# Keeping four engines of a DeltaNet and FFN kernel in program order, with the first stages regrouped

## The chip, the cores and the metric

One core of a Trainium2 chip runs the whole kernel. Time is device microseconds (us) of that core. Runs of one kernel agree within about one per cent. Kernels are compared only within the same rounds. The kernel before took 722.61 us (median of three runs, 721.08 to 725.26).

In the profile PE is TensorE (matmuls), PEld its weight loads, DVE is VectorE, ACT is ScalarE, POOL is GpSimd, SP is SyncE, whose queue here issues most DMAs. A line of an order of time reads: start in us, duration in us, engine, source line, operation, out<-in, shape, count, and in brackets the idle time just before it with what ended that.

## The reference

Two stages on 4 batches, 8 heads, 768 tokens, head size 48 (model width 384):

```python
k_n = k / (np.linalg.norm(k, axis=-1, keepdims=True) + 1e-06)
for t in range(S):                       # attention: a delta rule, token by token
    y[:, :, t] = einsum('bhd,bhde->bhe', q[:, :, t], state)
    v_old = einsum('bhde,bhd->bhe', state, kt)
    state = state + bt * einsum('bhd,bhe->bhde', kt, vt - v_old)
# x = y with the heads side by side, [4, 768, 384]
xn = (x - mean) / sqrt(var + 1e-06) * g_ln
out = x + maximum(xn @ w_ch1, 0.0) @ w_ch2      # 384 -> 1536 -> 384
```

The weights come as float64.

## The kernel before

The sequence is cut into 12 chunks of 64 tokens; two chunks make a slab. The program is written as Python generators, and a `Plan` decides in which order their steps are put out: `spread(gen, count, t0, t1)` puts the steps of a generator evenly between two points of a made-up time axis ("steps of the plan", meant to be about a microsecond). After that a scheduler is still free to reorder the instructions of each engine.

The parts that matter:

```python
def to_fp32(i):            # one "weight piece", 128x384 doubles: 6 VectorE instructions
    part  = (hi >> 13) & 0x3FF80
    power = max(part, ..) - ..
    man   = hi & 0xFFFFF | 0x100000
    full  = lo * 2**-32 + man
    full  = hi & 0x80000000 | full
    w_sb  = full * scale_w * power
# 24 pieces: 12 of w1, then 12 of w2

def prep(c):               # k, q transposed (p_t), gram matrices (p_g -> gsb, pt), gsb to DRAM (gd)
def blocks(m, engs):       # inverse of the diagonal blocks of a slab
    for ...: dma(gb, gd)                    # 8 small transfers back from DRAM
    yield
    nrm = sqrt(diagonal of gb)              # ScalarE: the "norms"
    nrm = 1/(nrm + 1e-6); db = nrm*nrm*beta; gb = gb*db; ...   # VectorE
    yield
    for j in range(31):                     # 31 pairs, each needs the one before
        tmp = xb[column j] * gb[row j]
        xb  = xb - tmp
        if j % 2: yield
    dma(xd, xb); for ...: dma(xt, xd)
    yield
def join(chunks):          # xn = transpose(xt) on VectorE; p_e, p_z on TensorE, ScalarE between
def recur(c, g):           # p_by, rhs, p_u, u, p_s, s, p_by, x_ln, LayerNorm (xn_ln), p_n
def ffn(c):                # 12 x (3 p_h, h_f); then, for each token group, 12 p_o

# ... the first stages (see the diff), then:
T = 45
starts = [0, 16, 84] + [114 + T * i for i in range(NCH - 2)]
plan.spread(join(range(2)), 5, -1, 0)
plan.spread(weights(6, NW // 2), NW // 2 - 6, 0, 20)
plan.spread(weights(NW // 2, NW), NW - NW // 2, 20, 52)
for c in range(NCH):
    plan.spread(in_turn(recur(c, 0), recur(c, 1)), 2 * N_RECUR, starts[c], ends[c])
...                                          # ffn(0): 12 to 32 and 48 to 64; ffn(1): 64 to 114
for c in range(2, NCH):
    plan.spread(ffn(c), N_FFN, starts[c + 1], starts[c + 1] + T)
for m in range(1, NSL):                      # slabs 1 to 5
    times = (t - 88, t - 62, t - 26, t - 8) if m > 1 else (4, 22, 62, 76)
    plan.spread(in_turn(*(prep(c) for c in chunks)), SLAB * N_PREP, times[0], times[1])
    plan.spread(blocks(m, (nc.sync,)), N_BLOCKS + 1, times[1], times[2])
    plan.spread(join(chunks), 5, times[3], t)
plan.run()
```

## Time and profile before

| what | us |
|---|---|
| first join (first xn on VectorE) | 107.2 |
| FFN of chunk 0 starts | 133.8 |
| second join (first p_e) | 201.9 |
| end of the trace | 719.1 |
| TensorE idle from 201.9 to the end | 37.9 |

This is the list of TensorE's waits of the kernel before from 201.9 to the end; the columns are us in total, times, and the longest.

```profile
PE p_e L392 <- DVE xn L384: 16.8, 4, 11.9
PE p_s L475 <- ACT u L432: 3.5, 5, 0.9
PE p_n L513 <- DVE xn_ln L506: 3.0, 4, 1.1
```

The one large wait is for the transposed inverse at the joins. The other waits of the list last at most 1.5 us each; they come to 16.9 us in sum, and the last matmul ends at 714.5, 4.6 us before the end.

### The profile page before, as it was taken

To read this page: it belongs to the slowest core of one execution; us is meant where nothing else is said; L and a number is where in the kernel's file an instruction comes from. 1 tells how busy PE (TensorE), PEld (TensorE's weight loads), DVE (VectorE), ACT (ScalarE), POOL (GpSimd) and SP (SyncE) were. 2 spreads that over 40 slices of the span, in tenths; PEclk is the share of its full clock that TensorE was granted. 3 is DMA by queue.
4 is the path that set the end of the run, shared out by engine and by line. 5 is a ranking of instruction groups with operands and counts; after the bars stand their busy time and mean duration, and the time that the engine had idled before them with its cause. 6 is when DMAs were issued, how large, how long until landed. Compare 5 with 4: busy or idle time off the path is not lost.

```text
span 719.1 us, 17676 instructions
## 1 busy us (share of the span) xinstructions
PE 586.0 (81%) x7784; PEld 433.2 (60%) x7784; DVE 355.7 (49%) x894; ACT 179.4 (25%) x452; POOL 59.9 (8%) x80
## 2 busy tenths in 40 slices
PE   1610008999998994799998899997999999999997
PEld 1410007776865762686765786765876757858684
DVE  4788997337735297311497313595212874021100
ACT  3200003531233221233221352222341312213120
POOL 5222440001000011000011000011000000000000
PEclk9999999999999898599999699998799997999999
DMA  8998261433034412113505023414012012000000
GB/s 148 199 192 143 71 168 47 90 75 60 30 64 101 68 34 68 28 30 91 79 3 122 7 64 70 67 25 103 2 46 56 14 45 39 1 12 13 12 12 22
DMA packets 135292, 45.28 MB, mean 63 GB/s; under 512 B 128304, under 2 KB 131376, under 8 KB 135216
## 3 DMA queue, kind: packets, MB, share of 16 engines
q1 hardware_dynamic: 126992, 33.80, 24.4%
q0 software_dynamic: 1920, 9.44, 4.7%
q10 hardware_dynamic: 6304, 0.92, 1.0%
q8 instruction: 61, 1.00, 0.6%
q14 instruction: 15, 0.12, 0.1%
HBM read 29.98 MB, written 14.16 MB: 61 GB/s over the span
## 4 chain that ended last, share of the span: by engine, by line
PE 54%; DVE 30%; DMA 7%; issue 3%; ACT 3%; SPq 2%; POOL 0%; DVEq 0%; ACTq 0%; POOLq 0%
PE p_h L526 19%; PE p_o L537 17%; DVE tmp L357 9%; DVE xb L362 8%; PE p_t L249 3%; PE p_g L260 3%; PE p_by L448 2%; DMA words<-in_moe_w_ch_dram 2%; PE p_z L412 2%; PE p_u L464 2%; PE p_e L392 2%; PE p_by L490 2%; SPq L116 1%; PE p_n L513 1%; PE p_s L475 1%
## 5 line engine op out<-in xcount | busy, mean ns | idle before, releaser
L526 PE MATMUL p_h<-xnt,w_sb 128*128 128x256 f32 x864 | 213.3, 397 | 1.3 <-ACT h_f L531 1.1
L537 PE MATMUL p_o<-w_sb,h_f 128*128 128x384 f32 x576 | 200.9, 494 | 0.0
L526 PEld LDWEIGHTS p_h<-xnt,w_sb 128*128 128x128 f32 x864 | 164.6, 198 | 28.7 <-ACT h_f L531 2.5
L537 PEld LDWEIGHTS p_o<-w_sb,h_f 128*128 128x128 f32 x576 | 104.9, 190 | 62.1 <-issue 0.5
L531 ACT ACTIVATE h_f<-p_h 128x256 f32<-128x256 f32 x144 | 55.0, 383 | 148.6 <-PE p_h L526 148.3
L392 PE MATMUL p_e<-xn,gsb 32*32 32x32 f32 x768 | 20.7, 218 | 73.3 <-DVE xn L384 73.3
L357 DVE TENSOR_TENSOR tmp<-xb,gb 128x31 f32<-128x31 f32 (+15 forms) x186 | 67.0, 360 | 4.3
L362 DVE TENSOR_TENSOR xb<-xb,tmp 128x31 f32<-128x31 f32 (+15 forms) x186 | 64.2, 345 | 4.5
L392 PEld LDWEIGHTS p_e<-xn,gsb 32*32 32x32 f32 x768 | 18.5, 132 | 76.6 <-DVE xn L384 73.0
L268 DVE TENSOR_TENSOR pt<-p_g,pmask 128x512 f32<-128x512 f32 x24 | 16.6, 690 | 79.7 <-ACT gsb L265 78.0
L260 PE MATMUL p_g<-kqt 48*64 48x128 f32 (+1 forms) x896 | 31.2, 287 | 26.6 <-DVE nrm L342 15.3
L260 PEld LDWEIGHTS p_g<-kqt 48*64 48x64 f32 x896 | 25.0, 157 | 34.2 <-ACT ksq L280 15.4
L544 DVE TENSOR_TENSOR o<-p_o,x_ln 128x384 f32<-128x384 f32 x24 | 13.4, 557 | 61.4 <-PE p_o L537 61.1
L481 DVE TENSOR_TENSOR s<-s,p_s 48x384 f32<-48x384 f32 x44 | 24.3, 552 | 23.7 <-PE p_s L475 23.0
L448 PEld LDWEIGHTS p_by<-s,kqt 48*64 48x64 f32 x1408 | 26.7, 143 | 13.1 <-issue 9.8
L453 DVE TENSOR_TENSOR rhs<-v_raw,p_by 128x384 f32<-128x384 f32 x22 | 12.1, 552 | 43.7 <-PE p_by L448 40.8
L400 ACT ACTIVATE es<-p_e 32x256 f32<-32x256 f32 x48 | 18.0, 375 | 61.4 <-PE p_e L392 55.7
L448 PE MATMUL p_by<-s,kqt 48*64 48x48 f32 x1408 | 31.5, 231 | 2.0 <-ACT x_ln L432 2.0
L250 ACT COPY kqt<-p_t 128x512 f32<-128x512 f32 x48 | 27.9, 585 | 19.2 <-PE p_t L249 12.6
L417 DVE COPY xt<-p_z 32x256 f32<-32x256 f32 x48 | 20.0, 417 | 25.3 <-PE p_z L412 24.8
L280 ACT ACTIVATE ksq<-kpad 128x384 f32<-128x384 f32 x24 | 12.5, 521 | 67.9 <-DVE ksum L281 51.1
L351 POOL COPY xb<-db 128x32 f32<-128x32 f32 x6 | 3.5, 584 | 273.9 <-DVE db L346 273.9
(68 smaller groups left out, 516.1 us busy)
## 6 DMA issues: line engine op xcount, KB each, us to landing
words<-in_moe_w_ch_dram POOLq DMA_DIRECT2D x24, 384.0 KB, 3.9
gd<-gsb SPq DMA_DIRECT2D x12, 512.0 KB, 3.2
qpad<-in_q_dram SPq DMA_DIRECT2D x24, 192.0 KB, 4.8
v_raw<-in_v_dram SPq DMA_DIRECT2D x24, 192.0 KB, 5.2
out_dram<-o SPq DMA_DIRECT2D x48, 96.0 KB, 2.2
kpad<-in_k_dram SPq DMA_DIRECT2D x22, 192.0 KB, 3.9
xd<-xb SPq DMA_DIRECT2D x6, 512.0 KB, 2.9
gb<-gd SPq DMA_DIRECT2D x44, 64.0 KB, 3.3
```

Source lines behind the costliest of these rows:

```text
L249: nc.tensor.transpose(p_t[:, j], src[:, h : h + 2], ident)
L250: nc.scalar.copy(made[c][0][g][:, :, n], p_t)
L260: nc.tensor.matmul(p_g[toks, hp, j, n0:n1], kqt[rows, j, 0, toks], kqt[rows, j, n0:n1, toks])
L357: nc.vector.tensor_tensor(out=t, in0=xb[:, 0:n, j : j + 1].to_broadcast([128, n, w]), in1=gb[:, j : j + 1, j + 1 : BK].to_broadcast([128, ...
L362: nc.vector.tensor_tensor(out=rest, in0=rest, in1=t, op=ALU.subtract)
L392: nc.tensor.matmul(p_e[r1, h % H], gsb[r0, h, BK:C], xn[r0, h])
L417: nc.vector.tensor_copy(out=xt[r0, g * H : (g + 1) * H, BK:C], in_=p_z[r0])
L448: nc.tensor.matmul(p_by[half(e ^ (hp & n)), hp, n, j], kqt[rows, j, n, half(e)], s[rows, e, j], start=(n == 0 and j == 0), stop=(n == 0), ...
L481: nc.vector.tensor_tensor(out=new, in0=new, in1=p_s[DP * hp : DP * hp + D, :, 0 : NP * D].rearrange("p e (j d) -> p e j d", d=D), op=ALU.add,)
L526: nc.tensor.matmul(p_h, w1_sb[:, t, f * 128 : (f + 1) * 128], xnt[:, t], start=(t == 0), stop=(t == KC - 1),)
L531: nc.scalar.activation(h_f, p_h, ACTF.Relu)
L537: nc.tensor.matmul(p_o, hs[f][:, g * 128 : (g + 1) * 128], w2_sb[:, f], start=(f == 0), stop=(f == FT - 1),)
```

## The change

The intent: the plan is made with care, so let the engines keep it. A context manager chains every instruction of VectorE, ScalarE, TensorE and the SyncE queue to the one before it on the same engine, with a dependency that the scheduler has to respect (GpSimd stays free). The first stages are regrouped to be good in just that order: the squares of k after the grams, only three weight pieces before the first inverse and none inside it, then values, products and the first join at once.

```diff
+@contextmanager
+def in_this_order(tc):
+    traced = tc.nc.cur_bb.bb.instructions
+    first = len(traced)
+    yield
+    last = {}
+    for ins in tc.nc.cur_bb.bb.instructions[first:]:
+        if ins.engine not in ORDERED:            # DVE, Activation, PE, SP
+            continue
+        if ins.engine in last:
+            tc.add_manual_dep(ins, last[ins.engine],
+                mybir.DependencyInfo(NoSync, DATA), reason="in_this_order")
+        last[ins.engine] = ins.name
...
-    first.spread(weights(0, 5), 5, 0, 8)
-    first.run()
-    inverse = blocks(0, (nc.sync, nc.scalar))
-    next(inverse)
-    ...                                   # loads of q and v of chunks 0, 1
-    for _ in inverse:
-        pass
-    ...                                   # prep_p of chunks 0, 1 (scale_v on GpSimd, q transposed, products)
-    first.spread(weights(5, 6), 1, 3, 4)
+    order.enter_context(in_this_order(tc))
+    first.spread(weights(0, 3), 3, 0, 8)
+    first.run()
+    knrms = [norms(c) for c in two]
+    inverse = blocks(0, (nc.sync, nc.scalar))
+    next(inverse)
+    ...                                   # loads of q and v of chunks 0, 1
+    next(inverse)
+    ...                                   # q transposed; loads of chunks 2, 3
+    for _ in inverse:
+        pass
+    for c in two:
+        scale_v(c, knrms[c], nc.vector)
+        for g in two:
+            products(c, g, 1, 2)
+    for _ in weights(3, 5):
+        pass
+    for _ in join(two):
+        pass
...
-    plan.spread(join(range(2)), 5, -1, 0)
-    plan.spread(weights(6, NW // 2), NW // 2 - 6, 0, 20)
+    plan.spread(weights(5, NW // 2), NW // 2 - 5, 0, 20)
...
     plan.run()
+    order.close()
```

## The prediction

> **What bounds the kernel now.** I read the page first (busy shares, the 40 slices), then the six stretches below, then the order of time within them.
>
> ```profile
> PE 586.0 (81%) x7784; PEld 433.2 (60%) x7784; DVE 355.7 (49%) x894; ACT 179.4 (25%) x452; POOL 59.9 (8%) x80
> ...
> PE   1610008999998994799998899997999999999997
> ...
> DVE  4788997337735297311497313595212874021100
> ...
> PEclk9999999999999898599999699998799997999999
> ```
>
> TensorE (PE) is nearly idle for the first 108 us and nearly full later; VectorE (DVE) is the reverse. The share of 81% hides two programs with two limits. The stretches, columns PE, weight load, DVE, ACT, POOL busy, granted clock, DMA share, GB/s:
>
> ```profile
> 0.00:36.10 36.10, 14.75 (x224) 11.78 (x224) 21.63 (x47) 11.61 (x21) 13.07 (x31) 1.00 0.89 173
> 36.10:50.30 14.20, 1.13 (x32) 0.97 (x32) 10.81 (x27) 0.77 (x2) 2.29 (x6) 1.00 1.24 193
> 50.30:96.90 46.60, 1.13 (x32) 0.97 (x32) 44.79 (x127) 1.90 (x5) 19.46 (x15) 1.00 0.55 114
> 96.90:133.80 36.90, 22.53 (x550) 19.07 (x550) 26.01 (x58) 9.78 (x25) 3.10 (x5) 1.00 0.43 100
> 133.80:201.90 68.10, 67.08 (x710) 50.38 (x708) 38.10 (x96) 20.65 (x52) 4.73 (x6) 1.00 0.30 64
> 201.90:719.10 517.20, 479.33 (x6242) 350.06 (x6242) 214.33 (x542) 134.72 (x348) 17.21 (x19) 0.93 0.21 44
> ```
>
> At 36.1 the norms of the first blocks exist (ACT nrm); DVE takes them up at 48.0 because weight pieces stand ahead of them. From 50.3 to 96.9 DVE runs the first inverse (31 pairs tmp, xb) interleaved one for one with ten weight pieces. The first join starts at 107.2, the FFN of chunk 0 at 133.8, with all weights converted. From there PE is full but for some waits: in the last stretch it is idle 517.2-479.3 = 37.9 us and then cold (clock 0.50 for some 10 us after each of four joins).
>
> Costs of single things are read from the order of time:
>
> ```profile
> 97.21 0.42 DVE L206 TENSOR_SCALAR part<-words 128x384 uint32<-128x384 uint32 x1
> 97.67 0.38 DVE L211 TENSOR_SCALAR power<-part 128x384 uint16<-128x384 uint32 x1
> ...
> 101.14 0.50 DVE L206 TENSOR_SCALAR part<-words 128x384 uint32<-128x384 uint32 x1 [0.85 <-DMA words<-in_moe_w_ch_dram]
> ...
> 371.13 0.42 DVE L357 TENSOR_TENSOR tmp<-xb,gb 128x255 f32<-128x255 f32 x1
> 371.58 0.42 DVE L362 TENSOR_TENSOR xb<-xb,tmp 128x255 f32<-128x255 f32 x1
> ...
> 352.68 2.86 PE L526 MATMUL p_h<-xnt,w_sb 128*128 128x256 f32 x12
> 355.46 0.68 PE L464 MATMUL p_u<-rhs,xt 64*64 64x48 f32 x32
> 356.08 2.86 PE L526 MATMUL p_h<-xnt,w_sb 128*128 128x256 f32 x12
> ...
> 335.31 0.34 SPq L305 DMA_DIRECT2D gd<-gsb  x1
> ...
> 338.32 2.29 SPq L335 DMA_DIRECT2D gb<-gd  x4
> ```
>
> A weight piece alone costs 101.14-97.21-0.85 = 3.07 us. A dependent inverse instruction costs its duration plus 0.036; the whole inverse alone is (67.0+64.2)/6 + 62*0.036 = 24.1 us. Interleaved, ten pieces and the inverse (30.7+24.1+4 ksum) took 46.6: neighbours that don't depend on each other overlap by nearly 0.1 us. A p_h record costs 1.30/6 = 0.2155 us in a run, a p_o record 0.3225, so one FFN is 72*0.2155+48*0.3225 = 31 us, and each return to the FFN from small matmuls about 0.2 more (2.78 against 2.59).
>
> **What the Trainium skill says.** "TensorE: Matmul & The Clock Gate", the table at its head: TensorE's queue is 64 deep and can only pull weight loads ahead; VectorE, ScalarE and GpSimd are strict FIFO. The trace agrees: the norms of 36.1 waited until 48.0 behind pieces that needed their own words. So the order of issue decides, and that is what changes. "VectorE: DVE Perf Modes", section "The DRAIN you can't avoid": the next op starts only when the pipe is empty, but one that isn't held starts earlier. The trace shows the difference as 3.07 us against about 2.3 us a piece. "TensorE: Matmul & The Clock Gate", Part 1: an idle window of about 3.4 us halves the clock; the trace agrees (0.50 and 0.56 at 280 to 300, after 10 us idle). "DMA: Bandwidth & Descriptors", anatomy section: about 2 us fixed per transfer; here gb took 2.7 to 5.6 us, so gd and then gb cost 8 to 9 us from the copy to use.
>
> **The change part by part.** The edges forbid the scheduler to reorder PE, DVE, ACT and the SP queue; POOL stays free. No arithmetic is removed. Two scale_v move from POOL to DVE.
>
> First stages. ACT no longer puts the squares first, so the grams go out near 18 instead of 24.9, but the gb transfers of ACT's queue stand behind the norms of k, which wait for three pieces and four ksum on DVE (about 27). Norms at about 35, hardly better than 36.1. Then DVE goes on at once: 2.4 + 24.1 = 61.5 for the inverse, against 96.9. Next, on DVE's own order, scale_v 2*0.95, four pt with a gram each between (p_g is single-buffered), two pieces 6.1: 13.8, so xn at 75.3 (before: 107.2). Here 32 us are won. The join in strict order alternates PE, ACT, DVE four times with a cold PE: about 13.5, against 10.7. The recurrence starts at about 88.8.
>
> The bill. Nineteen pieces (5 to 23) remain and now stand between the recurrences of chunks 0 and 1 and the second inverse. Piece 23 comes after pair 24 of that inverse. DVE from 88.8: 19*3.07 = 58.3; 24 pairs 19.9; norms and gb 2.3; four recurrence halves 14.0; rhs, ksum, pt 6.4; sum 100.9, less 3 for overlap, plus about 9 for waits on PE and ACT (u, s, rstd): 107. Last weight at 196. PE reaches p_o of chunk 0 at about 160, and each of its twelve steps needs one w2 piece, so it trickles to 196; the second token group takes 24*0.3225 = 7.7: 204. The second join starts at about 212 behind 18 p_h; before it started at 201.9, with nearly all of chunk 1's FFN already done.
>
> The rest. From 204 PE has 11*31 = 341 FFN, 10 chunks of recurrence at 6.26 = 62.6, prep of 8 chunks 30, joins 22, and 159 returns to the FFN at 0.2 = 32: 487.6. The same count for before from 201.9 gives 9+310+62.6+28+22+124*0.2 = 456; measured were 517.2, less 37.9 idle, less about 24 for cold stretches = 455. The count holds to a per cent. So 204+490 = 694 plus waits.
>
> Waits. In the new order norms follow the last p_g of a slab by a few positions, while the data need gsb 0.8, gd 3, gb issue 2.3, gb 3: 9.3 us. On chunk 2, rhs stands behind norms on DVE: PE has 7.2 us of work and p_u comes at 12.7. For later slabs p_n follows a LayerNorm that stands behind norms, gb, s and ten pairs; DVE gets there at 20, PE at 14. With DVE's backlog (34 us of work for 30 to 37 of PE) I get 14 us for the second slab and 13 for each of three more, cold clock included, and 1.5 elsewhere: 54. The joins themselves become nearly free, since p_o is kept back between their steps. I take three quarters, 41, as such walks count each wait in full. 694+41 = 735.
>
> **Rivals.** (a) The gain carries through: join 23 us or more earlier, the rest as before: 696. For it: chunk 0 does start earlier, and before's four cold joins go. Against: the 19 pieces; DVE was the full engine of 50 to 107 and its work isn't less. (b) Strict order smooths PE so well that waits fall to 20: 714. For: between joins before ran 10.00 of 10 us busy in much this order. Against: the 9.3 us to norms, which the scheduler had hidden by placing them 20 us after gsb (334.7 to 354.6). (c) Waits in full and a slower weight phase: 755 to 760. For: DVE and PE now wait on each other with nothing to slip in.
>
> **Range and chances.** Last weight 196 +-7, waits 41 +-15: 708 to 760 for 8 in 10, middle 735. Over 2% faster means below 708.2: needs both at their best, 0.12. Slower by over 2% means above 737.1: 0.46. Within: 0.42.
>
> **What would show it.** Right: first xn near 75; inverse without weight instructions between, some 24 us; last w_sb write near 196; PE busy under half from 90 to 195; second join after 205; idle PE before p_u or p_n just after each norms; no cold joins. Wrong: last w_sb well before 180; p_o of chunk 0 not trickling; norms without idle PE, which would give (b); or PE full from 130 on, which would give (a).

## The result, and the profile after

The changed kernel took 761.31 us (757.49 to 763.1, four runs) beside 723.79 us of the kernel before on the same chip (721.08 to 725.26). The ratio is 1.0516, 95% interval 1.0461 to 1.0571: slower. Ratios here and below are the mean time of one kernel's fast runs over that of the other's fast runs of the same rounds, so they are not quite the ratio of the medians quoted.

First the busy shares and slices of the page after:

```profile
span 760.3 us, 17663 instructions
...
PE   4102358462689769989969999599999599999997
...
DVE  3496667789613278333395423692331963221100
...
PEclk9965559876599989999989999899999899999999
```

TensorE starts earlier than before and is then half busy until slice 11 (209 us; slices count from 0), where before it was full from slice 6 (108 us). Later on there are four slices marked 5 or 6 (from 266, 380, 475 and 589 us), where the kernel before had one, marked 4, from 270 us.

The same cuts as in the prediction, placed at the events of the changed kernel (columns: stretch and its length, then busy time and count of PE, weight load, DVE, ACT, POOL, then granted clock, DMA share, GB/s):

```profile
0.00:33.90 33.90, 8.27 (x144) 6.92 (x144) 13.10 (x29) 9.83 (x17) 11.66 (x28) 1.00 0.75 145
33.90:73.20 39.30, 7.83 (x144) 6.58 (x144) 33.20 (x86) 2.34 (x4) 1.31 (x3) 0.60 0.97 125
73.20:85.00 11.80, 6.76 (x288) 5.98 (x288) 4.83 (x12) 3.01 (x8) 1.17 (x2) 0.50 0.13 36
85.00:199.80 114.80, 57.42 (x747) 41.23 (x747) 91.58 (x210) 21.06 (x55) 13.34 (x22) 0.69 0.29 73
199.80:211.50 11.70, 11.70 (x27) 6.71 (x28) 4.03 (x16) 0.00 (x0) 0.95 (x1) 0.74 0.42 98
211.50:760.30 548.80, 489.57 (x6436) 347.96 (x6434) 218.97 (x549) 139.47 (x368) 17.66 (x23) 0.96 0.26 46
```

The granted clock of the first stretches should not be compared with the 1.00 that the prediction shows for the kernel before: there p_s on 32 matmuls took 0.89 us at 118.65, against 0.57 at full clock (in the changed kernel at 370.06), so TensorE ran at half speed where the view says 1.00.

Up to 85 us the change does what it was made for: the norms are there at 33.9, the inverse runs alone, the first join starts at 73.2 instead of 107.2. Then the bill: for 115 us TensorE is half idle, while VectorE has 92 us of work. In the last stretch, TensorE is idle 548.80-489.57 = 59.2 us; before, 37.9 after 201.9.

The order of time on TensorE at the end of the fourth stretch shows why it stands:

```profile
179.74 1.65 PE L551 MATMUL p_o<-w_sb,h_f 128*128 128x384 f32 x2 [5.45 <-DVE w_sb L249]
184.38 1.65 PE L551 MATMUL p_o<-w_sb,h_f 128*128 128x384 f32 x2 [2.99 <-DVE w_sb L249]
...
199.78 11.69 PE L551 MATMUL p_o<-w_sb,h_f 128*128 128x384 f32 x26 [4.55 <-DVE w_sb L249]
...
222.38 0.69 PE L406 MATMUL p_e<-xn,gsb 32*32 32x32 f32 x32 [0.27 <-ACT kqt L271]
```

Each pair of p_o waits for one w2 piece. The last group is 26 matmuls (2 of the first token group, 24 of the second). It lasts 11.69 us, where 26 at the 0.3225 us of the prediction would last 8.4: the granted clock in it is 0.74 on average, 0.50 up to 206.0 and 1.00 after that. The second join starts at 222.4, before at 201.9.

TensorE's waits from 222 to the end, the same columns as before:

```profile
PE p_n L527 <- DVE xn_ln L520: 27.3, 7, 8.2
PE p_u L478 <- DVE rhs L467: 6.6, 2, 6.3
PE p_s L489 <- DVE pt L289: 4.3, 3, 1.4
PE p_h L540 <- ACT h_f L545: 3.9, 4, 1.0
PE p_n L527 <- ACT es L414: 3.6, 4, 0.9
PE p_t L270 <- ACT es L414: 2.6, 2, 1.7
PE p_g L281 <- DVE s L495: 1.3, 1, 1.3
PE p_e L406 <- DVE xn L398: 1.3, 4, 0.3
```

The wait for xn at the joins is gone from the top of the list (it is 1.3 us, before 16.8). In its place stands p_n, which waits for the LayerNorm. Five long waits, all soon after the norms of a slab, come to 32.5 us: two at the second slab, shown next, and one at each of the three later ones (7.29 us at 386.67, 7.85 at 491.83, 8.22 at 599.05).

```profile
269.53 1.10 PE L478 MATMUL p_u<-rhs,xt 64*64 64x48 f32 x32 [6.29 <-DVE rhs L467]
...
282.00 0.55 PE L527 MATMUL p_n<-ident,xn_ln 128*128 128x128 f32 x3 [2.80 <-DVE xn_ln L520]
```

The first of the later ones, in the order of time of all engines from 365 to 388:

```profile
365.92 0.34 SPq L329 DMA_DIRECT2D gd<-gsb  x1
...
366.36 5.75 SPq L349 DMA_DIRECT2D gb<-gd  x8
...
375.21 0.26 ACT L355 ACTIVATE nrm<-gb 128x32 f32<-128x32 f32 x1 [6.74 <-DMA gb<-gd]
...
375.51 0.18 DVE L356 TENSOR_SCALAR nrm<-nrm 128x32 f32<-128x32 f32 x1 [7.38 <-ACT nrm L355]
...
386.14 0.48 DVE L520 TENSOR_SCALAR xn_ln<-x_ln,mv,rstd 128x384 f32<-128x384 f32 x1
...
386.67 0.90 PE L527 MATMUL p_n<-ident,xn_ln 128*128 128x128 f32 x3 [7.29 <-DVE xn_ln L520]
```

Read it from the top. The grams go to DRAM and come back; that takes 375.2-365.9 = 9.3 us. VectorE stands for 7.4 us, because the norms are next in its order. The LayerNorm stands behind them and behind the first pairs of the inverse, and TensorE, with the p_n of that LayerNorm next in *its* order, stands for 7.3 us in turn. The label of a wait names only the last link (xn_ln); the first cause is the transfer three links back. The second is the work that VectorE, once it goes on at 375.5, still does ahead of the LayerNorm: the rest of the norms, the product of gb, s, o and eight pairs.

### The profile page after: what moved, and what is told of

Read it like the earlier page. It is cut to its first block, busy times and chain, and to the rows that moved or that the text cites. A ratio compares the mean times of both kernels' runs of the same rounds, so it can differ in the third digit from the quotient of the medians.

```text
span 760.3 us, 17663 instructions
## 1 busy us (share of the span) xinstructions
PE 581.5 (76%) x7784; PEld 415.4 (55%) x7784; DVE 365.7 (48%) x896; ACT 175.7 (23%) x452; POOL 46.1 (6%) x78
## 3 DMA queue, kind: packets, MB, share of 16 engines
q1 hardware_dynamic: 126992, 33.80, 26.7%
## 4 chain that ended last, share of the span: by engine, by line
PE 50%; DVE 32%; DMA 7%; ACT 4%; issue 3%; SPq 2%; ACTq 0%; DVEq 0%
PE p_o L551 19%; PE p_h L540 16%; DVE xb L376 7%; DVE tmp L371 7%; PE p_g L281 3%; DMA gb<-gd 3%; PE p_by L462 2%; DVE full L242 2%; DMA gd<-gsb 2%; DVE w_sb L249 2%; DMA kpad<-in_k_dram 2%; DVE full L245 2%; DVE s L495 2%; PE p_t L270 2%; SPq L349 2%
## 5 line engine op out<-in xcount | busy, mean ns | idle before, releaser
L551 PE MATMUL p_o<-w_sb,h_f 128*128 128x384 f32 x576 | 218.4, 521 | 21.4 <-DVE w_sb L249 21.4
L540 PEld LDWEIGHTS p_h<-xnt,w_sb 128*128 128x128 f32 x864 | 162.0, 195 | 32.0 <-ACT h_f L545 6.1
L551 PEld LDWEIGHTS p_o<-w_sb,h_f 128*128 128x128 f32 x576 | 108.4, 200 | 88.4 <-DVE w_sb L249 21.5
L371 DVE TENSOR_TENSOR tmp<-xb,gb 128x31 f32<-128x31 f32 (+15 forms) x186 | 63.2, 340 | 5.0
L281 PE MATMUL p_g<-kqt 48*64 48x128 f32 (+1 forms) x896 | 32.5, 295 | 30.2 <-DVE pt L289 23.7
L527 PE MATMUL p_n<-ident,xn_ln 128*128 128x128 f32 x72 | 14.6, 320 | 49.1 <-DVE xn_ln L520 45.6
L558 DVE TENSOR_TENSOR o<-p_o,x_ln 128x384 f32<-128x384 f32 x24 | 13.4, 557 | 59.9 <-PE p_o L551 59.7
L527 PEld LDWEIGHTS p_n<-ident,xn_ln 128*128 128x128 f32 x72 | 9.3, 159 | 55.7 <-DVE xn_ln L520 43.8
L270 PE MATMUL p_t<-ident,qpad 128*128 128x128 f32 x96 | 17.0, 313 | 21.7 <-DMA qpad<-in_q_dram 20.3
L271 ACT COPY kqt<-p_t 128x512 f32<-128x512 f32 x48 | 28.0, 584 | 20.6 <-PE p_t L270 20.0
L431 DVE COPY xt<-p_z 32x256 f32<-32x256 f32 x48 | 20.0, 417 | 22.1 <-PE p_z L426 21.4
L406 PEld LDWEIGHTS p_e<-xn,gsb 32*32 32x32 f32 x768 | 16.1, 114 | 22.0 <-DVE xn L398 9.8
L406 PE MATMUL p_e<-xn,gsb 32*32 32x32 f32 x768 | 19.0, 201 | 11.5 <-DVE xn L398 10.3
L478 PE MATMUL p_u<-rhs,xt 64*64 64x48 f32 x704 | 15.8, 230 | 15.3 <-DVE rhs L467 14.6
```

What stands on the lines that cost most here:

```text
L270: nc.tensor.transpose(p_t[:, j], src[:, h : h + 2], ident)
L271: nc.scalar.copy(made[c][0][g][:, :, n], p_t)
L281: nc.tensor.matmul(p_g[toks, hp, j, n0:n1], kqt[rows, j, 0, toks], kqt[rows, j, n0:n1, toks])
L371: nc.vector.tensor_tensor(out=t, in0=xb[:, 0:n, j : j + 1].to_broadcast([128, n, w]), in1=gb[:, j : j + 1, j + 1 : BK].to_broadcast([128, ...
L406: nc.tensor.matmul(p_e[r1, h % H], gsb[r0, h, BK:C], xn[r0, h])
L431: nc.vector.tensor_copy(out=xt[r0, g * H : (g + 1) * H, BK:C], in_=p_z[r0])
```

## The experiments

The kernels marked as edits "of the changed kernel" differ from it only by the lines shown.

### Which half of the change costs: the regrouping or the order

Regrouping without the order, an edit of the changed kernel:

```diff
-    order.enter_context(in_this_order(tc))
```

> The regrouped first stages, but no order edges: the scheduler may reorder every engine. Theory A (the strict order costs the time): the scheduler puts weight pieces between the instructions of the first inverse again, nine or ten of them, so the time is near that of the kernel before: 710 to 732 us, first xn near 100 to 107 us. Theory B (the regrouping pushed 19 pieces behind the first join and that costs the time): 745 us or more, last weight after 180 us.

The order without the regrouping: the kernel before, with the same context manager around its own first stages and plan.

```diff
+    order = ExitStack()
+    order.enter_context(in_this_order(tc))
     first = Plan()
     ...
     plan.run()
+    order.close()
```

> The kernel before with the order edges alone, its first stages as they were. Theory A: slower much like the full change, 745 to 775 us, with PE idle before p_u or p_n after each norms of slabs 2 to 5, and no weight piece between the instructions of the first inverse. Theory B: near the kernel before, 715 to 735 us.

Measured: regrouping alone 721.75 us (ratio 0.997, interval 0.9914 to 1.0026), order alone 761.12 us (1.0503, 1.0442 to 1.0565). The weight pieces show what is behind this. These are VectorE's writes of w_sb (ns min/median/max, then the first and last start in us), first of regrouping alone, then of order alone:

```profile
L249 DVE SCALAR_TENSOR_TENSOR w_sb<-full,scale_w,power x24: 602/614/1829, 15.9 to 121.5; 128x384 f32<-128x384 f32 x24
```

```profile
L249 DVE SCALAR_TENSOR_TENSOR w_sb<-full,scale_w,power x24: 617/619/619, 14.4 to 199.6; 128x384 f32<-128x384 f32 x24
```

Without the order the scheduler puts the pieces back into the first inverse whatever the source says, and they are done at 122; the first join is then at 106.5. With the order the last one starts at 199.6, and the first join starts at 78.0 even without the regrouping. So the whole loss belongs to the order, and so does most of the early start; the regrouping on its own does nothing that the interval can tell from zero.

### Where in the program the order costs

The order is kept on one side of step 64 of the plan, the step where the FFN of chunk 1 begins. Edits of the changed kernel:

```diff
# order up to the second join
-    plan.run()
-    order.close()
+    plan.once(64, order.close)
+    plan.run()

# order after it
-    order.enter_context(in_this_order(tc))
...
+    plan.once(64, order.enter_context, in_this_order(tc))
     plan.run()
     order.close()
```

> The changed kernel with its order kept only up to the step where the FFN of chunk 1 begins (step 64 of the plan); after that the scheduler is free. Theory (about half of the 38 us is the weight phase before the second join, about half the later slabs): last w_sb near 199 as in the changed kernel, p_e of the second join near 220, total 735 to 748. Rival (the later slabs cost all of it, since work put off in the weight phase is made up for by the free joins): 720 to 730.

> The reverse: the scheduler is free up to step 64 of the plan and the order is kept from there to the end. Theory: first join late (near 107) and last w_sb near 122 as without an order, the waits at the norms of the slabs come back (p_u and p_n on VectorE, 5 to 7 us at each), but the four joins run without long waits; total 735 to 748. Rival (the weight phase costs all): 720 to 728.

Measured: up to step 64, 738.67 us (1.022, 1.0171 to 1.0269), so 14.5 us over the 724.19 of before in these rounds; after it, 745.93 us (1.0306, 1.0253 to 1.0359), so 21.7 us over. Together 36.2, against 37.5 for the whole: the cost splits into two parts that add up.

The second part has waits of both sorts, those of the norms and one at the second join, which the expectation had not (TensorE's waits from 190 on):

```profile
PE p_n L527 <- DVE xn_ln L520: 26.1, 7, 7.7
PE p_e L406 <- DVE xn L398: 18.8, 5, 17.5
PE p_u L478 <- DVE rhs L467: 6.7, 1, 6.7
```

### The two costs repaired, one by one and together

Norms later. In slabs 2 to 5 the transfers of gb stay where they were, and the norms and the inverse come six steps later. An edit of the changed kernel:

```diff
-        plan.spread(blocks(m, (nc.sync,)), N_BLOCKS + 1, times[1], times[2])
+        inverse = blocks(m, (nc.sync,))
+        plan.spread(inverse, 1, times[1], times[1] + 2, whole=False)
+        late = 6 if m > 1 else 0
+        plan.spread(inverse, N_BLOCKS, times[1] + 2 + late, times[2] + late)
```

> The changed kernel, with norms and inverse of slabs 2 to 5 put out 6 plan units later than the transfers they wait for. If ACT and DVE stand in line behind the gb transfers (my theory for the waits of the later slabs): PE's idle time before p_u and p_n after norms, some 6 to 9 us a slab, goes, with its cold clock; about 35 us in all: 720 to 735 us. If the waits come from VectorE's backlog of inverse work instead, they only move: gain under 10 us, 752 us or more.

Measured 740.75 us (1.023, 1.0179 to 1.0282): 20.6 us won, but the expected time was missed by 6 us. TensorE's waits from 221 on show about half of the time for xn_ln (27.3 us) still there:

```profile
PE p_n L527 <- DVE xn_ln L520: 14.0, 11, 2.9
PE p_h L540 <- ACT h_f L545: 8.1, 4, 2.1
```

The long waits for xn_ln (up to 8.2 us each) are gone; eleven of up to 2.9 us remain, and the wait for h_f has doubled. In one of the eleven (p_n at 397.3) VectorE had copied x_ln at 392.3 and began its LayerNorm only at 395.5, with pairs of the inverse between.

Weights early. Ten weight pieces go into the first inverse, instruction by instruction, as the scheduler had done. An edit of the changed kernel, with the generators made to yield after every instruction:

```diff
-        for _ in inverse:
-            pass
+        pieces_too = weights_fine(3, 13)
+        for _ in inverse:
+            next(pieces_too, None)
+        for _ in pieces_too:
+            pass
...
-        for _ in weights(3, 5):
-            pass
...
-    plan.spread(weights(5, NW // 2), NW // 2 - 5, 0, 20)
-    plan.spread(weights(NW // 2, NW), NW - NW // 2, 20, 52)
+    plan.spread(weights(13, NW), NW - 13, 0, 40)
```

> The changed kernel, with ten weight pieces put instruction by instruction between those of the first inverse, in strict order; eleven pieces remain after the first join. If the serial weight pieces after the join hold back the FFN (my theory for the first 210 us): first xn later, near 92 us instead of 73, but last weight near 177 instead of 199.6 and no p_o that waits for w_sb; 735 to 750 us. Rival: the late join shifts all that follows and gives the gain back: 756 to 765 us.

Measured 751.42 us (1.0387, 1.0335 to 1.044): 9.9 us won, a little less than expected. The first xn moves from 73.2 to 86.4, the last w_sb from 199.0 to 182.1, and TensorE's wait for w_sb shrinks from 21.4 us in six waits to 0.9 in one. So a first join 13 us later made the kernel faster.

Both:

> Both repairs at once: norms six steps later in the slabs from the second on, and ten weight pieces inside the first inverse. Theory (two separate costs, one in the later slabs and one in the weight phase): the gains add, 20.6 + 9.9, so 761.3 - 30.5 = 731, within 726 to 736. Rival (both are one stock of slack of TensorE, which can be won back only once): 738 to 742, no better than norms late alone.

Measured 732.62 us (1.015, 1.0099 to 1.0201): 28.7 us below the changed kernel, against 20.6+9.9 = 30.5. Two separate costs, repaired separately.

### Which engine's order costs

Edits of the one line that names the ordered engines:

```diff
-ORDERED = tuple(getattr(mybir.EngineType, n) for n in ("DVE", "Activation", "PE", "SP"))
+ORDERED = tuple(getattr(mybir.EngineType, n) for n in ("DVE",))           # or ("PE",), or ("DVE", "PE")
```

> The changed kernel with the order kept on VectorE alone; TensorE, ScalarE and the queue are left to the scheduler. Theory (VectorE's place for the norms and for the weights is the cause; TensorE's own order only decides whether it can fill the wait): last w_sb late, 185 to 200, as in the changed kernel, but TensorE slips FFN matmuls into the waits of p_n and p_u, so 730 to 748. Rival (the cost is TensorE's rigid order): within 1.5% of the kernel before, 715 to 728.

> The order kept on TensorE alone. Theory (VectorE's order is the cause): with VectorE free the scheduler puts weight pieces inside the first inverse and the norms where their data are there, so last w_sb near 122 to 130, waits at norms under 10 us in sum, 715 to 730. Rival (TensorE's rigid order is the cause): 745 or more, with p_n and p_u waits as in the changed kernel.

> The order kept on TensorE and VectorE, with ScalarE and the queue left to the scheduler. Alone the order of VectorE cost 2 us and that of TensorE 11. Theory (the cost is the product of the two: VectorE late by its own order, and TensorE unable to fill the wait by its own): nearly the whole of it, 752 to 764. Rival (the order of ScalarE or of the queue, which neither of those runs had, makes the difference): 730 to 742, near the sum of 2 and 11 above the kernel before.

Measured, each against the kernel before in its own rounds:

| ordered | us | before | more | ratio (95%) |
|---|---|---|---|---|
| VectorE | 725.27 | 723.32 | 2.0 | 1.0037 (0.9986 to 1.0089) |
| TensorE | 734.51 | 723.32 | 11.2 | 1.0154 (1.0108 to 1.0199) |
| both | 751.52 | 721.43 | 30.1 | 1.0433 (1.0405 to 1.0461) |
| all four | 761.31 | 723.79 | 37.5 | 1.0516 (1.0461 to 1.0571) |

My theory, that VectorE's order is the cause and would be seen with VectorE alone, fell here: that kernel has the late weights (last w_sb at 196.6) and the order of the norms, and it costs nothing that the interval can tell from zero. TensorE alone came between the two expectations. Its waits are others than those of the changed kernel: from 190 on only 0.3 us for xn_ln, but this for xn at the joins, where the kernel before had 16.8:

```profile
PE p_e L406 <- DVE xn L398: 27.8, 8, 12.0
```

The 11 us more of this wait are about what the run costs; whether a gap at the joins that TensorE may no longer fill is all of it, no run shows. Both together, just below the 752 to 764 expected, cost more than twice their sum.

TensorE's order of time with VectorE alone ordered shows how the same late weights are taken:

```profile
186.54 2.93 PE L551 MATMUL p_o<-w_sb,h_f 128*128 128x384 f32 x4 [1.70 <-DVE w_sb L249]
191.13 2.93 PE L551 MATMUL p_o<-w_sb,h_f 128*128 128x384 f32 x4 [1.66 <-DVE w_sb L249]
197.25 2.29 PE L551 MATMUL p_o<-w_sb,h_f 128*128 128x384 f32 x4 [3.19 <-DVE w_sb L249]
200.46 4.74 PE L540 MATMUL p_h<-xnt,w_sb 128*128 128x256 f32 x11 [0.93 <-DVE o L558]
```

Each w2 piece is used for both token groups at once (x4 instead of x2), so the group of 24 that followed at 199.78 in the changed kernel is not there, and p_h of chunk 1 starts at 200.5 instead of 211.3. And the norms' long waits are not there either. TensorE's waits from 222 on, with VectorE alone ordered, then with both:

```profile
PE p_n L527 <- DVE xn_ln L520: 13.9, 10, 3.0
PE p_by L462 <- ACT x_ln L446: 6.8, 4, 3.9
PE p_u L478 <- DVE rhs L467: 2.0, 1, 2.0
```

```profile
PE p_n L527 <- DVE xn_ln L520: 25.8, 7, 6.8
PE p_u L478 <- DVE rhs L467: 6.3, 1, 6.3
PE p_s L489 <- DVE pt L289: 4.3, 3, 1.4
```

So most of the loss needs both: a VectorE that is late by its own order, and a TensorE that may not do anything else meanwhile. The remaining 37.5-30.1 = 7.4 us, taken from different rounds, come with the order of ScalarE and of the SyncE queue; which of the two, no run tells.

### A version that beats both kernels

If the scheduler is good where engines are unequally loaded and the plan is good in the steady part, each should have its part. First the order from step 64 on, with the norms late:

> The same free first part, strict order from step 64 on, and norms six steps later in the slabs from the second on. Theory (first part costs nothing if left to the scheduler, later part loses little once the norms don't stand ahead of their data): the run before minus some 20, so 715 to 728, near or a little below the kernel before. Rival (norms late wins only where TensorE has fallen behind): 735 or more.

Measured 726.9 us (1.0031, 0.9971 to 1.009): the late norms win 19.0 us here as well, and it is level with the kernel before. TensorE's waits from 190 on name the rest:

```profile
PE p_e L406 <- DVE xn L398: 18.9, 5, 17.6
PE p_n L527 <- DVE xn_ln L520: 12.9, 10, 2.9
```

The 17.6 us are one wait, at the second join: the order starts just before it, so TensorE may not put the FFN of chunk 1 ahead. Let it start at step 84 instead, with chunk 2:

```diff
-    plan.once(64, order.enter_context, in_this_order(tc))
+    plan.once(84, order.enter_context, in_this_order(tc))
```

> As the run with a free first part and late norms, but the scheduler stays free up to step 84 of the plan, the start of chunk 2, so that TensorE may put FFN matmuls of chunk 1 ahead of the second join, where that run waited 17.6 us for xn. Theory (that wait is the last large one): p_e of the second join starts with under 8 us of idle time, 709 to 720, below the kernel before. Rival (the work slipped in there is missing later, where the strict order can't replace it): 722 to 730.

Measured 713.96 us (710.44 to 717.3), ratio 0.9877, interval 0.9819 to 0.9934. It is the fastest kernel here, 1.2% below the kernel before and 6% below the changed one; a difference counts as faster or slower only from 2% on, so it still counts as the same as before. The wait it was made for, of TensorE from 190 on:

```profile
PE p_e L406 <- DVE xn L398: 9.7, 6, 8.1
```

The longest wait for xn fell from 17.6 to 8.1 us (just over the 8 expected), and the time by 12.9 us.

## Why the prediction was wrong

It said 735, with 708 to 760 for eight in ten; measured were 761.3, just beyond the range and in the tail of its most likely class ("slower", 0.46). Step by step:

- **First stages.** Right. Norms at 33.9 (said 35), end of the first inverse 59.9 (61.5), xn 73.2 (75.3), join 11.7 us (13.5).
- **The bill.** Right in kind, a little short. The last piece was written at 199.6 (said 196), with 91.6 us of VectorE work in the 114.8 us from 85 on; p_o of chunk 0 trickled as said; TensorE was busy for half of the stretch.
- **The second token group of chunk 0.** Mis-sized by 7.5 us: "24*0.3225 = 7.7: 204", but it ended at 211.5. Of this 3.6 us are the later last weight, 0.6 that the group had 26 matmuls, and 11.69-8.4 = 3.3 the clock, at 0.50 for the first 6.2 us of the group. The prediction counted cold clock in the later waits, but not here.
- **The work after that.** The number agrees (490 used, 489.6 us busy), but by luck: the prediction counted work at full clock, and the measured time contains half speed. An estimate from windows of 1 us (busy time in each, times one minus its clock) gives 12.8 us for that, so 476.8 at full clock, 13 us less than the count.
- **The waits at the norms.** Right in kind; right in size too, but by luck. The walk gave 14+3*13 = 53 us, cold clock included. TensorE stood for 6.29+2.80+7.29+7.85+8.22 = 32.5 us, and the slow clock after these waits cost about 7.7 more, by the same estimate: 40.2, close to the 41 taken. The reason given, "as such walks count each wait in full", was not it: at the three later slabs the idle time was longer than the walk had it (7.3 to 8.2 us for 20-14 = 6), and the cold clock cost far less (1.4 to 2.1 us).
- **"And 1.5 elsewhere".** This is the step that failed. TensorE was idle for 59.2 us from 211.5 on, so 26.7 of them outside the five waits: about 22 in waits of at most 1.7 us each, and 4.5 between the last matmul (it ends at 755.75) and the end. The slow clock outside the norms, about 5 us, was left out as well. The kernel before shows that most of this was there to be read: of its 37.9 us of idle time the joins' waits were 16.8, and about 21 were such small waits and the end. The prediction let all 37.9 go, since the joins would become free, and put 1.5 in their place.

The sum closes: the start is 211.5 instead of 204, which is 7.5; work at full clock 476.8 instead of 490, which is -13.2; waits and slow clock 32.5+7.7+26.7+5.1 = 72.0 instead of 41, which is 31.0. 735+7.5-13.2+31.0 = 760.3, the span of the trace.

Of the rivals, (c), "waits in full and a slower weight phase: 755 to 760", comes nearest in the number. The weight phase was slower, but the waits at the norms were not the walk's in full (40.2 of 53); the small ones made up for it. Of (b), that joins become nearly free, that much was true (xn: 16.8 to 1.3 us), but the norms took its place. (a) fell with the second join at 222.4.

Redone, the other sums of the prediction hold, with small slips: 1.30/6 is 0.2167, not 0.2155, and "about 2.3 us a piece" leaves the four ksum inside the 46.6 us, so it is less. Its remark that the trace agrees on the clock holds from 280 to 300, but not before: from 60 to 100 the same trace shows TensorE idle at a granted clock of 1.00, and the matmuls after it ran at half speed (see above).

What the prediction did not ask at all is what the runs made of the cause. It priced VectorE's order and looked for gaps in TensorE as a consequence. The runs with one engine ordered show that late weights and early norms on VectorE cost almost nothing as long as TensorE may fill the gap. The question for each wait is "may TensorE do something else here?", and in the changed kernel the answer is no.

## What to carry to other kernels

Fixing the issue order of VectorE alone cost next to nothing (2.0 us), as TensorE worked round its waits, and that of TensorE alone 11.2; fixing both, which feed each other, cost 30.1. When you price such a change, count the many small waits too, from the list of the kernel before, and not only the long ones that you can follow: here they were 22 us. A fixed order pays where the plan knows more than the scheduler (here the joins of the steady part, worth 1.2%), and only once each step stands behind its data by the measured time of its transfer, 9.3 us here; where loads are uneven, as in the first 200 us, leave it to the scheduler. An earlier first event is worth nothing if the work put off for it stands in the way of the next: here the first join came 34 us earlier and the second 20 us later.

## What the Trainium skill lacked or had wrong

- "TensorE: Matmul & The Clock Gate", Part 1, describes an idle window that halves the clock and about 3.4 us of sustained work that restores it. It also tells of kernels with short bursts between waits, but gives no share of busy time at which the clock falls. In the changed kernel it was 0.50 from 342.5 to 345.9, right after 3.4 us in which TensorE was busy for 1.97 us and waited once, for 1.43; the same again from 554.1 to 557.5. After a like stretch (445.3 to 448.7, also 1.97) it stayed at 1.00. And after a long wait the clock was back 2.9 us (599.05 to 601.9) to 6.2 us (199.8 to 206.0) after the first matmul.
- "DMA: Bandwidth & Descriptors", the anatomy section, gives about 2 us fixed per transfer for the path from GpSimd. No page has the whole way of a chain like the one here, a store to DRAM and then eight loads of 64 KB on SyncE's queue: 5.75 us to issue all eight and 8.85 us from the first issue to the norms that need them (366.36 to 375.21).
- No page: what it costs to fix the issue order on several engines at once. Here VectorE alone 2.0 us, TensorE alone 11.2, both 30.1, and with ScalarE and the SyncE queue 37.5.
